# Fused attention and gated FFN on one core: the opening in a new order, with clock fillers that read a constant

## The chip, the cores and the metric

The kernel runs on one core of one Trainium2 chip. The metric is the device time of one execution in microseconds (us). A profiled execution also has a span, which runs from its first to its last recorded event; the span is about 1.8 us shorter than the time of the same execution.

Single executions of one kernel scatter by some 0.3 us (standard deviation; one of 33 of the kernel before, at 226.29 us, lies farther off).

## The reference, cut to what matters

```
xread = softmax(x @ state.T / 8) @ state       # B=8, H=8, S=512, D=64
sread = softmax(state @ x.T / 8) @ x           # 32 state rows per head
x2    = concat(xread, sread) as (8 * 544, 512) rows
out   = (relu(x2 @ w_gate) * (x2 @ w_val)) @ w_out    # 512 -> 1536 -> 512
```

The result is float32. The products are computed in bfloat16.

## The kernel before

The kernel doesn't compute `xread` and then multiply it by the weights. For each batch it first builds `U`, the state times the gate and value weights, in units of 128, 256 or 512 weight columns. It then multiplies `U` by the transposed attention `ans`. One such "slice" is a batch and 128 of the 1536 inner columns: two gate products and two value products of 512 columns on TensorE (`gv`), a relu on ScalarE, and a multiply on VectorE. The output products (`o`) follow.

```
def u_unit(b, w, lo):                    # 512 columns of one weight, two PSUM banks
    ps = held["u", b, w, lo] = [bank("up"), bank("up")]
    u_mm(ps, b, w, lo, 512)
def c_unit(b, lo, n):                    # 128 or 256 columns, gate then value
    ps = [bank("upc")...  for kc in range(NK)]
    for w in range(2):
        u_mm([p[:, w] for p in ps], b, w, lo, n)
def gv(b, jf):
    held["gv", b, jf] = [bank("gv_ps"), bank("gv_ps")], hsb[b][:, jf], S
    for w in range(2):
        for kc in range(NK):
            gv_mm(held["gv", b, jf][0], b, jf, w, kc)
def mult(b, jf):                         # VectorE; frees the value bank
    nc.vector.tensor_tensor(out=dst, in0=ps[1][:, 0:n], in1=held["g", b, jf][:, 0:n], op=ALU.mult)
def att_scale(b, jp, eng="dve"):         # VectorE; both inputs in SBUF
    ...tensor_tensor(out=<a_sn>, in0=<e_sn>, in1=held["rc", b, jp].to_broadcast(...), op=ALU.mult)
def x_next(b):                           # GpSimd casts a whole batch of x, in two halves
    x_conv(b, 0, "pool")
    x_conv(b, 1, "pool")
    x_trans_dma(b)
def spin(n, cols=512):                   # fillers: keep TensorE busy while data is on its way
    for i in range(n):
        nc.tensor.matmul(warm_ps[:, 0:cols], warm[:, 0:128], warm[:, 0:cols], start=True, stop=True)
...
nc.vector.memset(warm, 0.0)
```

The first 28 slices, with all loads, transposes and `U` units among them, are issued by a hand-written program of words. Each engine takes its own words in the order given. `gv.1.8@21` is a slice (batch 1, inner part 8) whose gate goes to PSUM bank 2 and whose value goes to bank 1. `co`/`uo` are copies of `U` units out of PSUM, `nx` is `att_scale`, `xn` is `x_next`, `dw` are weight loads, and `sr` is the state read, on which nothing of the next slices depends. From slice 28 on a loop takes over, in both kernels the same.

The softmax here doesn't subtract the row's maximum and nothing guards it: scores larger than these inputs give would overflow.

## Time and profile before

| | before |
|---|---|
| time, median of 3 | 224.28 us (224.14 to 224.79) |
| the profiled execution | 224.73 us, span 222.9 us |
| TensorE busy | 217.4 us, 98% of the span |
| TensorE on the chain that ended last | 95% |
| full clock from | 10.21 us |
| first gate product | 15.12 us |
| start of slice 28, the loop's first | 56.44 us |

TensorE has almost no idle time after the first gate product, so the date of slice 28 decides the end. Behind it both kernels issue the same stream, and the span moves by what slice 28 moves, unless a later wait absorbs it. The prediction below shows the page, the chain and the timeline from which this is read. Columns: start, length, engine, line, operation, out<-in, sizes, count, and in brackets the idle time before and what ended it.

```profile
17.05 0.29 PE L291 MATMUL upc<-wv_sb,stT 64*32 64x256 bf16 x8
...
39.73 0.68 DVE L219 TENSOR_TENSOR a_sn<-e_sn,rc 128x512 bf16<-128x512 bf16 x1
40.70 2.02 POOL L142 CAST xb<-xf 128x1024 bf16<-128x1024 f32 x2 [4.96 <-DMA xf<-in_x_dram]
```

The value weights landed at 15.41 us and were wanted at 17.05, so they were early. The product took 0.68 us and was over 0.29 us before the two casts began.

### The profile page before, as it was taken

Reading aid. Unit: us, or ns where it says so; the run is one execution under the profiler, and the core shown is the slowest. Engines: PE = TensorE matmul, PEld = TensorE weight load, DVE = VectorE, ACT = ScalarE, POOL = GpSimd, SP = SyncE. Lnnn points to the kernel's source line nnn. Section 1 sums busy time; section 2 is a strip of 40 time slices with the busy share of each in tenths; the row PEclk is TensorE's granted clock in tenths of the full one; section 3 lists DMA queues with packets and bytes.
Section 4 is the critical chain, followed back from the end, with each engine's and each line's share of the span. In section 5 each row is a group of like instructions: output and inputs, shape, how many; then the busy total and the mean of one; then the engine's idle time right before and its main releaser. Section 6 shows DMA issues by size and latency. Waiting matters only on the chain.

```text
span 222.9 us, 4842 instructions
## 1 busy us (share of the span) xinstructions
PE 217.4 (98%) x1959; PEld 106.9 (48%) x1959; DVE 131.1 (59%) x233; ACT 123.2 (55%) x233; POOL 48.9 (22%) x54
## 2 busy tenths in 40 slices
PE   6999999999999999999999999999999999999994
PEld 2554454444544444444444444444444445666543
DVE  2399998965695559664877368646875433222100
ACT  4498788843567555574466456645654444222221
POOL 8877654300603334015000700000000000000000
PEclk9999999999999999999999999999999999999999
DMA  6999999152046771771169114511311111111132
GB/s 154 183 195 197 208 232 284 39 121 97 0 124 209 119 260 62 164 247 50 50 134 281 56 50 97 97 47 47 94 50 47 47 49 50 49 69 72 51 94 94
DMA packets 37799, 25.48 MB, mean 114 GB/s; under 512 B 18864, under 2 KB 33200, under 8 KB 37776
## 3 DMA queue, kind: packets, MB, share of 16 engines
q1 hardware_dynamic: 24912, 16.85, 26.3%
q0 software_dynamic: 11968, 7.47, 21.5%
q10 hardware_dynamic: 896, 0.85, 1.5%
q8 instruction: 15, 0.25, 0.4%
q14 instruction: 8, 0.07, 0.1%
HBM read 18.35 MB, written 8.91 MB: 122 GB/s over the span
## 4 chain that ended last, share of the span: by engine, by line
PE 95%; ACT 2%; DMA 1%; issue 0%; DVE 0%; DVEq 0%; ACTq 0%
PE o_ps L353 39%; PE gv_ps L316 38%; PE gv_ps L333 5%; PE up L291 4%; PE sc_ps L200 2%; DMA st_f<-in_state_dram 1%; PE sr_ps L264 1%; PE upc L291 1%; PE o_ps L379 1%; PE warm_ps L432 1%; PE xT_ps L186 1%; PE stT_ps L129 1%; PE xT_ps L169 1%; PE xT_ps L173 0%; ACT xT L189 0%; ACT e_sn L207 0%
## 5 line engine op out<-in xcount | busy, mean ns | idle before, releaser
L316 PE MATMUL gv_ps<-ans,U 128*128 128x512 bf16 x384 | 94.6, 379 | 0.3 <-ACT ans L249 0.3
L353 PE MATMUL o_ps<-wo_sb,h_sb 128*128 128x512 bf16 x372 | 94.8, 379 | 0.0
L340 ACT ACTIVATE g_sb<-gv_ps 128x512 bf16<-128x512 f32 (+1 forms) x108 | 62.5, 581 | 50.1 <-PE gv_ps L316 39.1
L344 DVE TENSOR_TENSOR h_sb<-gv_ps,g_sb 128x512 bf16<-128x512 f32 x96 | 64.7, 688 | 41.5 <-ACT g_sb L340 40.7
L316 PEld LDWEIGHTS <-U 128*128 128x128 bf16 x384 | 36.1, 98 | 40.7 <-issue 0.9
L353 PEld LDWEIGHTS <-h_sb 128*128 128x128 bf16 x372 | 35.3, 98 | 40.0 <-issue 1.6
L361 ACT COPY o_sb<-o_ps 128x512 f32<-128x512 f32 x29 | 17.1, 590 | 16.2 <-PE o_ps L353 16.2
L301 ACT CAST U<-up 128x512 bf16<-128x512 f32 x37 | 19.2, 594 | 11.1 <-PE up L291 11.1
L301 DVE CAST U<-up 128x512 bf16<-128x512 f32 x35 | 22.0, 682 | 2.3 <-PE up L291 1.9
L142 POOL CAST xb<-xf 128x1024 bf16<-128x1024 f32 x10 | 10.1, 1042 | 55.7 <-DMA xf<-in_x_dram 48.4
L256 POOL COPY xa<-xb 128x2048 bf16<-128x2048 bf16 (+1 forms) x9 | 15.6, 1748 | 13.9 <-issue 13.7
L213 DVE TENSOR_REDUCE cs<-e_sn 128x16 f32<-128x512 bf16 x16 | 10.9, 678 | 8.9 <-ACT e_sn L207 8.9
L344 DVE TENSOR_TENSOR hs_sb<-gv_ps,g_sb 128x256 bf16<-128x256 f32 x12 | 5.1, 425 | 15.3 <-PE gv_ps L333 10.5
L207 ACT ACTIVATE e_sn<-sc_ps 128x512 bf16<-128x512 f32 x16 | 9.7, 604 | 4.7 <-PE sc_ps L200 4.6
L219 DVE TENSOR_TENSOR a_sn<-e_sn,rc 128x512 bf16<-128x512 bf16 x16 | 11.4, 723 | 0.3
L291 PEld LDWEIGHTS <-stT 64*32 64x32 bf16 x512 | 5.9, 90 | 9.5 <-issue 8.1
L311 ACT CAST U<-upc 128x512 bf16<-128x512 f32 (+1 forms) x18 | 8.7, 542 | 0.9 <-PE upc L291 0.9
L200 PEld LDWEIGHTS <-xT 128*128 128x128 bf16 x128 | 5.9, 102 | 3.7 <-ACT xT L189 0.4
L291 PE MATMUL up<-wg_sb,stT 64*32 64x512 bf16 x144 | 7.5, 381 | 0.0
L432 PE MATMUL warm_ps<-hs_sb 128*128 128x512 bf16 x15 | 6.2, 548 | 1.2 <-DVE hs_sb L396 1.2
L333 PE MATMUL gv_ps<-br,wg_sb 128*128 128x256 bf16 x48 | 7.2, 273 | 0.0
L333 PE MATMUL gv_ps<-br,wv_sb 128*128 128x256 bf16 x48 | 7.2, 273 | 0.0
(65 smaller groups left out, 126.9 us busy)
## 6 DMA issues: line engine op xcount, KB each, us to landing
out_dram<-o_sb SPq DMA_DIRECT2D x31, 256.0 KB, 2.4
xf<-in_x_dram SPq DMA_DIRECT2D x4, 1024.0 KB, 6.1
wo_sb<-in_moe_w_out_dram POOLq DMA_DIRECT2D x2, 768.0 KB, 14.7
wg_sb<-in_moe_w_gate_dram POOLq DMA_DIRECT2D x5, 256.0 KB, 8.7
wv_sb<-in_moe_w_val_dram POOLq DMA_DIRECT2D x5, 256.0 KB, 9.3
xf<-in_x_dram POOLq DMA_DIRECT2D x1, 1024.0 KB, 15.4
xb<-in_x_dram POOLq DMA_DIRECT2D x3, 256.0 KB, 6.0
xb<-in_x_dram POOLq DMA_DIRECT2D x1, 512.0 KB, 11.7
```

Of the source, the lines that this page charges most:

```text
L200: nc.tensor.matmul(ps[:, :, c, jj], xT[b][:, c, 2 * jp + jj], stT[:, b, 2 * jp + jj], start=True, stop=True)
L213: nc.vector.reduce_sum(out=cs, in_=e_v, axis=AX.X)
L219: {"dve": nc.vector, "pool": nc.gpsimd}[eng].tensor_tensor(out=by_pair(a_sn[b], jp).rearrange("p r (j n) -> p r j n", n=Ns), in0=e_v, in1= ...
L256: nc.gpsimd.tensor_copy(out=v[:, hs:hs + src.shape[1]], in_=src)
L291: nc.tensor.matmul(dst[parity][32 * j:32 * j + 32], stT[r:r + 64, b, j, 32 * parity:32 * parity + 32], wsb[r:r + 64, j, lo:lo + n], start= ...
L301: copy[eng](out=U[b][:, w, kc, lo:lo + 512], in_=held["u", b, w, lo][kc])
L316: nc.tensor.matmul(ps[w], U[b][:, w, kc, f0:f0 + 128], ANS[b][:, kc].rearrange("p c t -> p (c t)"), start=(kc == 0), stop=(kc == NK - 1))
L333: nc.tensor.matmul(ps[w][:, 0:nt], wsb[:, j, f0:f0 + 128], br[:, j].rearrange("p b n -> p (b n)"), start=(j == 0), stop=(j == NJ - 1))
L340: nc.scalar.activation(out=g_sb[:, 0:n], in_=ps[0][:, 0:n], func=AF.Relu)
L344: nc.vector.tensor_tensor(out=dst, in0=ps[1][:, 0:n], in1=held["g", b, jf][:, 0:n], op=ALU.mult)
L353: nc.tensor.matmul(held["o", b, tsub], src[:, jf, tsub * 128:(tsub + 1) * 128], wo_sb[:, jf], start=(jf == 0), stop=(jf == NF - 1))
L361: copy[eng](out=o_sb, in_=held["o", b, tsub])
```

## The change

The intent is an earlier start. The fillers no longer wait for a memset, since they read a constant of ones that is there from the beginning, broadcast from one column. Some have 256 columns, to fit smaller gaps. And the words of the first 28 slices are put into a new order, made for the durations as they now are. `turn` only sets which bank the loop's outputs begin with.

```
-    warm = hs_sb.rearrange("p f n -> p (f n)")[:, 0:512]
-    given, turn = [], {"r": 0, "o": 0}
+    given, turn = [], {"r": 0, "o": 1}
-    nc.vector.memset(warm, 0.0)
+    one = nc.const_aps.tensor(1.0, (128, 1), BF16)
-            nc.tensor.matmul(warm_ps[:, 0:cols], warm[:, 0:128], warm[:, 0:cols], start=True, stop=True)
+            nc.tensor.matmul(warm_ps[:, 0:cols], one.to_broadcast([128, 128]), one.to_broadcast([128, cols]), start=True, stop=True)
     program = """
-    dx.1.0.2 dx.1.1.2 stc.0.0.act stc.0.1.dve xc.0.0.act dw.0.0.128 spin.6 stT.0@5 xT.0.0@0 ...
+    dx.1.0.2 dx.1.1.2 stc.0.0.act stc.0.1.dve dw.0.0.128 xc.0.0.dve spin.8 xT.0.0@0 ...
     (cut: words up to the second slice)
-    gv.0.1@42 ... c.0.256.256@17 c.1.256.256@65 co.0.256.256.1.act co.0.256.256.0.dve aT.1.0@3 aT.1.1@4 ...
+    gv.0.1@53 ... c.0.256.256@67 co.1.128.128.0.act aT.1.0@0 ... c.1.256.256@15 aT.1.1@4 ...
     (cut: words of slices 2 to 19)
-    ... nx.2.0 ... sc.2.1@5 o.0.1 uo.2.0.512.0.act xn.3 ...
+    ... nr.2.0 gv.1.8@21 ex.2.1 xn.3 re.1.8 nx.2.0 o.0.2 mu.1.8 u.2.0.0@04 of.0.0.act nr.2.1 u.2.1.0@35 u.2.1.512@21 ...
     (cut: words of slices 21 to 26)
-    gv.2.3@23 mu.2.1 re.2.3 o.0.9@7 mu.2.3 sr.0@4 sr.1@5 sn.0 sn.1 xp.2 xp.3
+    ... o.0.9@6 mu.2.2 u.2.0.512@42 sr.0@3 uo.2.0.512.1.act sr.1@5 sn.0 uo.2.0.512.0.act sn.1 xp.2 xp.3
```

More of the change, by code (lines that the diff above doesn't have):

```diff
@@ L441 @@
     program = """
-    dx.1.0.2 dx.1.1.2 stc.0.0.act stc.0.1.dve xc.0.0.act dw.0.0.128 spin.6 stT.0@5 xT.0.0@0 xc.0.1.dve dw.1.0.128 on
-    sto.0.dve xT.0.1@4 xo.0.0.dve dw.0.128.128 xo.0.1.act dw.1.128.128 dw.0.256.256 spin.4 xT.0.3@2 dw.1.256.256
-    xT.0.2@3 xo.0.3.dve sc.0.0@1 xo.0.2.act ex.0.0 sc.0.1@6 dw.0.512.256 xT2.1.0@5 ex.0.1 nr.0.0 xo2.1.0.act
-    dw.1.512.256 spin.2 xT2.1.1@0 nr.0.1 xo2.1.1.act sc.1.0@4 dw.0.768.256 nx.0.0 dw.1.768.256 ex.1.0 spin.2
-    c.1.0.128@23 nx.0.1 sc.1.1@1 co.1.0.128.1.act c.0.0.128@65 co.1.0.128.0.dve dw.0.1024.256 aT.0.1@0 ex.1.1
@@ L447 @@
-    co.0.0.128.0.dve aT.0.0@4 co.0.0.128.1.act ao.0.1.dve dw.1.1024.256 ao.0.0.act spin.1 c.1.128.128@32 nr.1.1
-    c.0.128.128@16 co.1.128.128.1.act gv.0.0@50 co.0.128.128.0.act nr.1.0 co.0.128.128.1.act dw.0.1280.256 re.0.0
-    gv.0.1@42 co.1.128.128.0.act nx.1.1 re.0.1 nx.1.0 dw.1.1280.256 c.0.256.256@17 c.1.256.256@65 co.0.256.256.1.act
-    co.0.256.256.0.dve aT.1.0@3 aT.1.1@4 co.1.256.256.0.act ao.1.0.dve gv.0.2@71 dx.2.0.1 ao.1.1.dve
-    co.1.256.256.1.act mu.0.1 re.0.2 gv.1.0@36 mu.0.0 ds re.1.0 mu.0.2 c.1.512.256@45 c.0.512.256@27
@@ L452 @@
-    co.1.512.256.0.act co.1.512.256.1.dve gv.1.1@03 co.0.512.256.1.act do.0.6 co.0.512.256.0.dve re.1.1 gv.1.4@14
-    mu.1.0 xp.0 re.1.4 gv.1.3@57 mu.1.1 re.1.3 mu.1.4 gv.0.5@20 mu.1.3 do.6.12 re.0.5 gv.0.3@61 mu.0.5 xp.1 re.0.3
-    c.0.768.256@35 c.0.1024.256@47 mu.0.3 co.0.768.256.1.act gv.1.2@20 co.0.1024.256.1.act co.0.768.256.0.dve df.3
-    re.1.2 gv.0.4@61 co.0.1024.256.0.dve re.0.4 mu.1.2 gv.1.5@57 mu.0.4 re.1.5 gv.0.9@32 mu.1.5 re.0.9 gv.0.8@46
-    mu.0.9 re.0.8 c.1.1280.256@01 c.0.1280.256@57 mu.0.8 co.1.1280.256.1.act xT2.2.1@3 co.0.1280.256.1.act
@@ L457 @@
-    co.1.1280.256.0.dve xT2.2.0@2 stc.1.0.pool co.0.1280.256.0.act c.1.768.256@46 xo2.2.1.dve stc.1.1.pool
-    c.1.1024.256@17 xo2.2.0.act stc.3.0.pool gv.1.10@05 co.1.768.256.0.dve stc.2.0.pool co.1.768.256.1.dve
-    co.1.1024.256.1.act stc.2.1.pool stT.1@3 gv.1.11@42 stc.3.1.pool re.1.10 sto.1.dve co.1.1024.256.0.act mu.1.10
-    gv.0.11@76 re.1.11 re.0.11 mu.1.11 gv.1.7@30 mu.0.11 re.1.7 gv.1.9@15 mu.1.7 re.1.9 sc.2.0@4 gv.0.7@72 mu.1.9
-    ex.2.0 re.0.7 nr.2.0 gv.0.6@36 re.0.6 mu.0.7 gv.0.10@01 mu.0.6 re.0.10 u.2.0.0@45 u.2.1.512@73 nx.2.0
@@ L462 @@
-    uo.2.0.0.1.act u.2.0.512@20 o.0.0@6 mu.0.10 uo.2.0.512.1.act uo.2.1.512.0.act uo.2.0.0.0.dve sc.2.1@5 o.0.1
-    uo.2.0.512.0.act xn.3 uo.2.1.512.1.dve ex.2.1 u.2.1.1024@01 nr.2.1 u.2.1.0@42 uo.2.1.1024.0.act u.2.0.1024@35
-    o.0.2 uo.2.1.0.1.act uo.2.0.1024.1.dve uo.2.1.0.0.act o.0.3@7 nx.2.1 of.0.0.dve aT.2.1@0 gv.1.8@25
-    uo.2.1.1024.1.dve ao.2.1.act re.1.8 uo.2.0.1024.0.dve aT.2.0@4 o.0.4 ao.2.0.dve mu.1.8 gv.2.0@01 re.2.0 o.0.5
-    mu.2.0 gv.2.2@23 of.0.1.act re.2.2 gv.1.6@45 mu.2.2 re.1.6 o.0.6@6 mu.1.6 o.0.7 o.0.8 gv.2.1@01 of.0.2.dve re.2.1
@@ L467 @@
-    gv.2.3@23 mu.2.1 re.2.3 o.0.9@7 mu.2.3 sr.0@4 sr.1@5 sn.0 sn.1 xp.2 xp.3
+    dx.1.0.2 dx.1.1.2 stc.0.0.act stc.0.1.dve dw.0.0.128 xc.0.0.dve spin.8 xT.0.0@0 xc.0.1.dve dw.1.0.128 on
+    xo.0.0.dve spin.1.256 xT.0.1@2 dw.0.128.128 stT.0@1 xo.0.1.act dw.1.128.128 sto.0.dve spin.1 spin.1.256 sc.0.0@3
+    dw.0.256.256 xT.0.2@5 ex.0.0 xT.0.3@4 dw.1.256.256 xo.0.2.dve xo.0.3.act nr.0.0 dw.0.512.256 spin.2 sc.0.1@6
+    xT2.1.0@0 ex.0.1 nx.0.0 xo2.1.0.act nr.0.1 dw.1.512.256 spin.2 xT2.1.1@2 xo2.1.1.act dw.0.768.256 sc.1.0@1 nx.0.1
@@ new lines @@
+    dw.1.768.256 spin.1 c.0.0.128@35 ex.1.0 aT.0.0@4 co.0.0.128.0.dve sc.1.1@6 co.0.0.128.1.act ao.0.0.dve aT.0.1@0
+    dw.0.1024.256 ex.1.1 c.1.0.128@21 nr.1.0 ao.0.1.act dw.1.1024.256 spin.1 c.0.128.128@35 c.1.128.128@46
+    co.1.0.128.0.act nr.1.1 co.0.128.128.1.act spin.2 gv.0.0@02 co.0.128.128.0.act co.1.128.128.1.act nx.1.0
+    dw.0.1280.256 re.0.0 gv.0.1@53 nx.1.1 co.1.0.128.1.act re.0.1 mu.0.0 dw.1.1280.256 c.0.256.256@67
+    co.1.128.128.0.act aT.1.0@0 co.0.256.256.0.act co.0.256.256.1.dve c.1.256.256@15 aT.1.1@4 ao.1.0.dve
@@ new lines @@
+    co.1.256.256.1.act gv.0.2@26 dx.2.0.1 mu.0.1 ao.1.1.act co.1.256.256.0.act gv.0.3@70 re.0.2 ds gv.1.2@53 re.0.3
+    mu.0.2 re.1.2 mu.0.3 c.1.512.256@41 do.0.6 c.0.512.256@27 co.1.512.256.1.act mu.1.2 gv.1.1@65 co.0.512.256.1.act
+    xp.0 co.1.512.256.0.dve re.1.1 gv.1.0@01 co.0.512.256.0.dve re.1.0 mu.1.1 c.0.768.256@37 c.1.768.256@46 do.6.12
+    gv.1.5@20 mu.1.0 co.1.768.256.1.act co.1.768.256.0.dve re.1.5 xp.1 gv.1.4@51 co.0.768.256.0.dve re.1.4 gv.1.3@62
+    co.0.768.256.1.dve re.1.3 mu.1.4 df.3 gv.1.7@43 mu.1.5 re.1.7 gv.0.4@57 mu.1.3 re.0.4 mu.1.7 gv.0.5@61 mu.0.4
@@ new lines @@
+    re.0.5 gv.0.7@04 mu.0.5 re.0.7 c.1.1280.256@25 c.0.1280.256@37 mu.0.7 co.1.1280.256.1.act c.0.1024.256@61
+    xT2.2.0@0 co.0.1024.256.0.act co.0.1024.256.1.dve xT2.2.1@4 co.0.1280.256.0.act stc.1.0.pool co.0.1280.256.1.dve
+    gv.0.9@56 xo2.2.0.act xo2.2.1.dve stc.1.1.pool gv.0.6@13 co.1.1280.256.0.dve re.0.9 re.0.6 stc.2.0.pool mu.0.9
+    gv.0.8@74 mu.0.6 re.0.8 stc.3.0.pool gv.0.11@05 mu.0.8 re.0.11 stc.2.1.pool gv.1.6@21 mu.0.11 re.1.6 stc.3.1.pool
+    stT.1@6 gv.0.10@73 mu.1.6 sto.1.act re.0.10 c.1.1024.256@40 u.2.1.1024@52 mu.0.10 co.1.1024.256.1.act
@@ new lines @@
+    u.2.0.1024@61 o.0.0@7 co.1.1024.256.0.act uo.2.1.1024.0.dve uo.2.1.1024.1.act uo.2.0.1024.0.dve gv.1.10@03
+    uo.2.0.1024.1.act re.1.10 sc.2.0@4 o.0.1 ex.2.0 mu.1.10 sc.2.1@5 nr.2.0 gv.1.8@21 ex.2.1 xn.3 re.1.8 nx.2.0 o.0.2
+    mu.1.8 u.2.0.0@04 of.0.0.act nr.2.1 u.2.1.0@35 u.2.1.512@21 uo.2.0.0.0.act o.0.3@6 uo.2.1.512.1.act uo.2.0.0.1.dve
+    uo.2.1.512.0.act o.0.4 nx.2.1 uo.2.1.0.0.act aT.2.1@0 uo.2.1.0.1.act aT.2.0@1 ao.2.1.dve o.0.5 ao.2.0.act
+    gv.2.0@42 of.0.1.act re.2.0 o.0.6@7 mu.2.0 gv.1.11@35 re.1.11 o.0.7 mu.1.11 gv.2.3@01 re.2.3 gv.2.1@42 mu.2.3
@@ L468 @@
+    re.2.1 o.0.8 mu.2.1 gv.1.9@35 of.0.2.dve re.1.9 gv.2.2@01 mu.1.9 re.2.2 o.0.9@6 mu.2.2 u.2.0.512@42 sr.0@3
+    uo.2.0.512.1.act sr.1@5 sn.0 uo.2.0.512.0.act sn.1 xp.2 xp.3
     """
```

## The prediction

> **What bounds the kernel now.** I read the page first, then the chain of waits in order of time, then the timeline of the first 18 us, because the change touches nothing after the first 28 slices but what these leave behind. The page:
>
> ```profile
> PE 217.4 (98%) x1959; PEld 106.9 (48%) x1959; DVE 131.1 (59%) x233; ACT 123.2 (55%) x233; POOL 48.9 (22%) x54
> PE 95%; ACT 2%; DMA 1%; issue 0%; DVE 0%; DVEq 0%; ACTq 0%
> ```
>
> TensorE is the engine of the end, busy 98% of the span and 95% of the chain that ended last. A busy figure with modelled ends can hide stalls, so I compared the start-to-start times of its products with the 216 ns that a 512-column product takes when full (20 in 4.42 us, below). From 15.12 us to the end I find three sorts of excess only: about 93 ns at each change between full products and those on part of the array, one wait of 0.20 us at 17.9 us, and the last output. So every microsecond by which the first gate product (line 316) comes sooner is a microsecond of the end, unless a later wait takes it back. The chain in time:
>
> ```profile
> 0.72 3.17 DMA st_f<-in_state_dram
> 4.54 0.61 PE stT_ps L129 x4
> 5.16 1.16 PE xT_ps L169 x8
> 6.32 1.71 PE warm_ps L432 x4
> 8.03 1.02 PE xT_ps L173 x9
> 9.71 0.61 PE sc_ps L200 x8
> 12.03 1.01 ACT xT L189
> 15.12 1.89 PE gv_ps L316 x8
> 20.62 4.42 PE gv_ps L316 x20
> ```
>
> Four fillers stand on the chain at 6.32 us, ahead of transposes whose input had landed (the transfer's semaphore is complete at 6.83 us). Later ScalarE carries the chain. The timeline of its first part:
>
> ```profile
> 1.18 2.74 PE L432 MATMUL warm_ps<-hs_sb 128*128 128x512 bf16 x6 [1.18 <-DVE hs_sb L396]
> 4.54 0.61 PE L129 MATMUL stT_ps<-id,st_b 128*128 128x128 bf16 x4 [0.63 <-ACT st_b L121]
> 7.96 1.06 PE L173 MATMUL xT_ps<-id,xb 128*64 128x128 bf16 x16
> 10.24 0.64 PE L186 MATMUL xT_ps<-id,xb 128*64 128x128 bf16 x16
> 10.93 2.12 ACT L189 COPY xT<-xT_ps 128x1024 bf16<-128x1024 bf16 x2
> 14.42 0.64 ACT L249 COPY ans<-aT_ps 128x512 bf16<-128x512 bf16 x1
> 15.12 1.89 PE L316 MATMUL gv_ps<-ans,U 128*128 128x512 bf16 x8 [0.26 <-ACT ans L249]
> ```
>
> The six fillers start after the memset, 427 ns apart: half speed. The same 16 transposes take 1.06 us at 7.96 us and 0.64 us at 10.24 us: full speed begins between them, and the trace's clock record puts it at 10.21 us.
>
> **What the Trainium skill says.** "TensorE: Matmul & The Clock Gate", Part 1, What's actually happening: the array runs at half clock until an activity window of some 3.4 us, free-running, was busy. The trace agrees in kind: half speed to 10.21 us, and a full-speed stretch of 211.63 us, 62 windows of 3.413 us. If the windows end at 3.4, 6.8 and 10.2 us here, the products' own time (427 ns a filler, 107 ns a transpose at half speed) covers some 65%, 68% and 85% of them; only the third released the clock, so the limit would lie between 68% and 85% in this run. Part 4 of that page, PE-mode transpose, says that transposes do not count as busy in the same way; without them the third window would be no fuller than the first, so this trace speaks for their counting. The page's head table gives ScalarE and VectorE a strictly ordered queue; the trace agrees, both carry out the program's order, and I use that below.
>
> **The change, part by part.**
> 1. Memset gone. VectorE loses 0.27 us. The fillers can start when the engines are released, about 0.8 us (VectorE's memset stands at 0.85), instead of 1.18. Eight of 427 ns end near 4.2 us, before the first transposes can start at 5.0 us (x lands at 4.47, its cast takes 0.47). So the two extra fillers cost nothing. They lift the coverage of the first window to about 76% ((3.38-0.8)/3.41) and of the second to 75%: inside my uncertain 68 to 85%. I give one half to full speed by 3.4 or 6.8 us.
> 2. Order up to the first gate product. The work ahead of it is the same: four score groups, two transposes of x[1], four small U units, two attention transposes. Fillers grow from 15 to 18 units of 512 columns (17 and two halves). The scores of head half 0 now come before the transposes of x's tail: state transposes end near 6.6 us, their copy near 7.2, scores 7.25 (before 8.96). Then, still at half clock, tail transposes to 8.5, ScalarE's exp to 8.5 and its copy of the second x pair to 9.36, second scores 9.4 (before 9.70), exp at 10.1, and the first 1024-element copy on ScalarE starts near 10.6 (before 10.93). From there ScalarE is full to the gate product, before and after: two large copies, two exps, then two small copies and the attention copy before, one small copy after. The timeline shows 4.13 us from 10.93 to 15.06; one small copy less (0.25 us apart) makes 3.85. Gate product at 14.5: 0.65 us sooner. With the clock released by 6.8 us the tail transposes end near 7.7, the second scores come at 8.5, the copy at 9.6, and the gate product at 13.5: 1.6 us sooner, of which some 0.15 us goes to the 256-column value weights that land at 15.41 us and would be wanted at 15.2.
> 3. From there to slice 28. Same 28 gate/value pairs and ten output parts. Changes between part-array and full-array work rise by my count from 16 to 18: +0.19 us. The wait of 0.20 us at 17.9 us probably goes: -0.20. The third x lands at 29.19 us; with 0.41 us of U work and changes moved ahead of it, its transposes are wanted at 30.05 or 29.3, so it just fits.
> 4. The hand-over. The new program ends with the U unit of batch 2, gate, columns 512, then two state-read groups (sr), and the first slice of the loop reads exactly those columns. In the built order this slice waits on ScalarE, which makes both copies, that of row half 1 first. For such a unit the timeline shows 39.56 us for its first product, and:
>
> ```profile
> 40.06 2.05 ACT L301 CAST U<-up 128x512 bf16<-128x512 f32 x4 [0.23 <-PE up L291]
> 55.81 0.71 PE L264 MATMUL sr_ps<-xa,e_sn 128*32 128x65 bf16 x64
> 56.45 1.04 PE L316 MATMUL gv_ps<-ans,U 128*128 128x512 bf16 x4
> ```
>
> The first copy starts 0.50 us after the unit's first product, the second 0.485 us later and takes 0.59: ready at 1.58, seen near 1.64. TensorE reaches the slice at 0.22 (unit) + 0.09 + 0.64 (sr and its change) = 0.95 us. It stands 0.69 us. Before, these columns were copied a dozen us earlier and gv followed sr with no wait. Nothing behind can absorb it: the stream is full to the end.
>
> Sum against the profiled run of 224.73 us, whose clock came late: late again -0.65 +0.19 -0.20 +0.69 = 0.0; early -1.45 +0.19 -0.20 +0.69 = -0.8, or 223.95. The faster runs of before (224.14, 224.28) I read as luckier windows; the change keeps their like at about 224.1.
>
> **Rivals.**
> A. No stall at the hand-over: the copies are in time or the order's author timed them well. Then -0.7 to -1.5: 223.2 to 224.0. Against it: both copies stand on one in-order engine, the first mm waits for the second of them, and an order made for the first 28 slices need not have counted what waits behind.
> B. The start does not move: ScalarE's run of copies or the DMA (busy tenths 9 from the second slice to the sixth) sets the gate product. Then only the additions stay, +0.7: 225.0. For it: ScalarE is busy 4.75 of the 5 us from 10 to 15. Against it: the run's own start moves, since the fillers and tail transposes no longer stand before the first scores.
> C. The fillers cost more: products reading one column over and over may not run at 427 and 216 ns. Eight have 0.8 us to spare, the nine behind have less; at 10% more, 0.2 us.
> D. A full-array product and no data may give a different window; the luck of the window alone moves a run by the 0.65 us that before's three runs span.
>
> **Range and chances.** The two halves of the clock question give 223.95 and 224.1 to 224.7; rival A pulls down, B up; I weigh A a little more, as such an order is usually kept for being faster. Predicted 224.0 us, 8 in 10 from 223.2 to 224.9. A change of 2% is 4.5 us, more than all idle and half-speed time I could remove, the 10.2 us of half clock being mostly waits for data: faster 0.01, within 2% 0.985, slower 0.005.
>
> **What would show it.** Right: fillers from about 0.8 us with no wait; first scores near 7.2 us; first gate product at 13.3 to 14.7 us; a wait of TensorE for ScalarE's U copy of some 0.7 us after sr near 55 us; no other wait beyond 0.3 us. Wrong: a gate product at 15 us or later (part 2), no wait after sr (part 4), new waits for weights or for the third x between 15 and 30 us (part 3), filler spacing off 427 or 216 ns (rival C).

## The result

| | before | after |
|---|---|---|
| time, median of 4 in the same rounds | 224.21 us (224.09 to 224.79) | 225.15 us (224.74 to 225.64) |
| ratio | | 1.0044 (95%: 1.0021 to 1.0067) |
| the profiled execution: time, span | 224.73, 222.9 us | 225.11, 223.3 us |

A ratio is the mean time of one kernel's runs over that of the other's of the same rounds, so it is not quite the ratio of the medians in the table. By the measure of 2% the two are the same. But the change is no gain: it costs something, and 225.15 lies outside the range of the prediction. With all runs together, the 33 of the kernel before have a mean of 224.56 us (median 224.50) and the 10 of the kernel after 225.00 (median 225.09), so the change costs about 0.5 us.

The page after, the lines for busy time and for the chain that ended last:

```profile
PE 213.8 (96%) x1934; PEld 106.1 (48%) x1963; DVE 130.2 (58%) x228; ACT 125.1 (56%) x237; POOL 49.4 (22%) x54
...
PE 85%; DMA 4%; POOL 3%; DVE 3%; issue 2%; ACT 2%; POOLq 0%; DVEq 0%
```

The fall of TensorE's busy time is not real. The trace has all 1963 weight loads and only 1934 products, 29 too few. At 216 ns each that is 6.3 us, more than the fall of 3.6, and each lost record leaves a gap that looks like a wait. A gap of 432 ns between two products' starts must therefore be checked against the weight loads before it is called one. The chain's shares are real news: DMA and VectorE are now on it. The chain after, in order of time:

```profile
7.66 8.38 DMA wv_sb<-in_moe_w_val_dram
17.65 2.32 PE gv_ps L315 x10
...
41.24 1.14 issue
42.38 0.69 DVE h_sb L343
43.67 1.67 PE o_ps L352 x7
```

It comes in by the value weights' transfer, which lands at 16.04 us. Near 41 us it goes over to VectorE: 1.14 us of "issue" (nothing that the profile shows as a wait; VectorE is inside the product `a_sn` then) and a multiply. The timeline of the kernel after says what these are. First the front:

```profile
0.76 3.57 PE L431 MATMUL warm_ps<-const-bfloat16-1.0 128*128 128x512 bf16 x8 [0.76 <-PEq L561]
6.25 0.39 PE L199 MATMUL sc_ps<-stT,xT 128*128 128x64 bf16 x8 [0.19 <-DVE stT L132]
...
13.67 1.89 PE L315 MATMUL gv_ps<-ans,U 128*128 128x512 bf16 x8
...
16.08 0.30 PE L290 MATMUL upc<-wv_sb,stT 64*32 64x256 bf16 x8 [0.28 <-DMA wv_sb<-in_moe_w_val_dram]
```

Eight fillers run from 0.76 us at once, the clock is full from 4.32 us on, and the first gate product comes at 13.67 us, 1.45 us before that of the other profile. Then TensorE comes to the 256-column value weights before they are there. Against its undisturbed course it loses 0.47 us (the bracket counts only idle time after the modelled end). Then the stretch near 42 us:

```profile
40.87 2.48 POOL L141 CAST xb<-xf 128x1024 bf16<-128x1024 f32 x2 [5.07 <-DMA xf<-in_x_dram]
40.98 1.47 DVE L218 TENSOR_TENSOR a_sn<-e_sn,rc 128x512 bf16<-128x512 bf16 x1
...
42.20 0.59 PE L290 MATMUL up<-wv_sb,stT 64*32 64x512 bf16 x9
42.38 0.68 DVE L343 TENSOR_TENSOR h_sb<-gv_ps,g_sb 128x512 bf16<-128x512 f32 x1
...
43.11 0.41 PE L290 MATMUL up<-wv_sb,stT 64*32 64x512 bf16 x7 [0.32 <-DVE h_sb L343]
```

The product `a_sn` now starts while GpSimd casts the fourth batch of x. It takes 1.47 us instead of 0.69. The multiply behind it (`mu.1.8`) is late by as much. That multiply empties bank 1, and the unit `u.2.1.512@21` wants bank 1. So the sixteen products of the two units (9 and 7) take 1.32 us, from 42.20 to 43.52, where 0.6 would do. Measured from start to start, TensorE loses 0.73 us. Last, the hand-over to the loop:

```profile
55.22 0.41 PE L290 MATMUL up<-wg_sb,stT 64*32 64x512 bf16 x8
55.56 0.70 PE L263 MATMUL sr_ps<-xa,e_sn 128*32 128x65 bf16 x64
55.70 1.07 ACT L300 CAST U<-up 128x512 bf16<-128x512 f32 x2 [1.07 <-PE up L290]
...
57.06 0.81 PE L315 MATMUL gv_ps<-ans,U 128*128 128x512 bf16 x3 [0.79 <-ACT U L300]
```

The first loop slice waits for the second of two copies of the unit that was made just before it. Its first product's record is one of the lost ones; its weight load stands at 56.83 us and shows the true start, 0.65 us after the slice could have begun.

From profile to profile the account is then closed (us, up to the start of slice 28):

| term | after minus before |
|---|---|
| first gate product 15.12 to 13.67 | -1.45 |
| wait for the value weights | +0.47 |
| bank wait behind VectorE's late multiply | +0.73 |
| two more changes between full-array and part-array products | +0.19 |
| the wait at 17.9 us of before, gone | -0.20 |
| hand-over wait | +0.65 |
| sum | +0.39 |
| slice 28 (weight loads at 56.44 and 56.83) | +0.39 |

The span differs by 0.38 us. Behind slice 28 nothing is gained or lost.

### The profile page after: what moved, and what is told of

Same layout as the page of the kernel before. It is cut to its first block, busy times and chain, and to the rows that moved or that the text cites. A ratio compares the mean times of both kernels' runs of the same rounds, so it can differ in the third digit from the quotient of the medians.

```text
span 223.3 us, 4821 instructions
## 1 busy us (share of the span) xinstructions
PE 213.8 (96%) x1934; PEld 106.1 (48%) x1963; DVE 130.2 (58%) x228; ACT 125.1 (56%) x237; POOL 49.4 (22%) x54
## 4 chain that ended last, share of the span: by engine, by line
PE 85%; DMA 4%; POOL 3%; DVE 3%; issue 2%; ACT 2%; POOLq 0%; DVEq 0%
PE o_ps L352 37%; PE gv_ps L315 34%; PE gv_ps L332 5%; PE up L290 4%; DMA wv_sb<-in_moe_w_val_dram 4%; DVE h_sb L343 1%; PE o_ps L378 1%; DVE U L310 1%; PE sc_ps L199 1%; PE sr_ps L263 1%; PE upc L290 1%; POOL wg_sb L109 1%; ACT U L300 1%; POOL xb L419 1%; POOL wv_sb L109 1%
## 5 line engine op out<-in xcount | busy, mean ns | idle before, releaser
L315 PE MATMUL gv_ps<-ans,U 128*128 128x512 bf16 x372 | 93.6, 379 | 1.3 <-ACT U L300 0.8
L352 PE MATMUL o_ps<-wo_sb,h_sb 128*128 128x512 bf16 x358 | 92.3, 379 | 1.9 <-issue 1.7
L300 ACT CAST U<-up 128x512 bf16<-128x512 f32 x39 | 20.4, 595 | 12.1 <-PE up L290 12.1
L360 ACT COPY o_sb<-o_ps 128x512 f32<-128x512 f32 x30 | 17.7, 590 | 16.4 <-PE o_ps L352 16.4
L141 POOL CAST xb<-xf 128x1024 bf16<-128x1024 f32 x10 | 10.6, 1088 | 56.3 <-DMA xf<-in_x_dram 36.7
L300 DVE CAST U<-up 128x512 bf16<-128x512 f32 x33 | 20.8, 682 | 2.3 <-PE up L290 1.9
L343 DVE TENSOR_TENSOR hs_sb<-gv_ps,g_sb 128x256 bf16<-128x256 f32 x12 | 5.1, 425 | 15.3 <-PE gv_ps L332 10.5
L218 DVE TENSOR_TENSOR a_sn<-e_sn,rc 128x512 bf16<-128x512 bf16 x16 | 12.3, 774 | 0.4
L290 PE MATMUL up<-wv_sb,stT 64*32 64x512 bf16 x144 | 7.4, 379 | 0.3 <-DVE h_sb L343 0.3
```

The source lines that it names most:

```text
L218: {"dve": nc.vector, "pool": nc.gpsimd}[eng].tensor_tensor(out=by_pair(a_sn[b], jp).rearrange("p r (j n) -> p r j n", n=Ns), in0=e_v, in1= ...
L290: nc.tensor.matmul(dst[parity][32 * j:32 * j + 32], stT[r:r + 64, b, j, 32 * parity:32 * parity + 32], wsb[r:r + 64, j, lo:lo + n], start= ...
L300: copy[eng](out=U[b][:, w, kc, lo:lo + 512], in_=held["u", b, w, lo][kc])
L315: nc.tensor.matmul(ps[w], U[b][:, w, kc, f0:f0 + 128], ANS[b][:, kc].rearrange("p c t -> p (c t)"), start=(kc == 0), stop=(kc == NK - 1))
L352: nc.tensor.matmul(held["o", b, tsub], src[:, jf, tsub * 128:(tsub + 1) * 128], wo_sb[:, jf], start=(jf == 0), stop=(jf == NF - 1))
L360: copy[eng](out=o_sb, in_=held["o", b, tsub])
```

## The experiments

**Theory.** The change's order wins time at the front, and two new waits, at 42 us and at the hand-over, take more than that. **Rivals.** The value weights set the pace, so that the front gain was never to be had. Or the front gain is the clock's luck in one profile of before. Or the new fillers are at fault. Twelve runs were made, in three jobs; the runs of the kernel before that each job shares have medians of 224.62, 224.66 and 224.55 us. The third job (b2_again, f1_again, h1_landed, g2_split) ran on another chip. The kernel before has a mean of 224.57 us in that job and, without the run at 226.29 us, 224.56 us in the other two, so the two chips are level. The table gives for each run the median, the ratio to before with its interval, and from its one profile when the clock was full, when the 256-column value weights landed, and when the first gate product, slice 14 and slice 28 started. Each interval is some 0.25 to 0.6% wide, and the mean of six runs is good to about 0.15 us.

| run | us (runs) | ratio (95%) | clock full | weights | gate | slice 14 | slice 28 |
|---|---|---|---|---|---|---|---|
| before, first profile | 224.21 (4) | | 10.21 | 15.41 | 15.12 | 32.09 | 56.44 |
| b2_again | 224.39 (6) | 0.9994 (0.9981-1.0008) | 4.25 | 16.34 | 13.92 | 31.42 | 56.06 |
| f1_ones8 | 224.56 (6) | 0.9991 (0.9964-1.0019) | 6.26 | 16.29 | 14.12 | 31.37 | 55.77 |
| f1_again | 224.29 (4) | 0.9990 (0.9977-1.0003) | 6.35 | 16.38 | 14.58 | 31.55 | 56.24 |
| after, first profile | 225.15 (4) | 1.0044 (1.0021-1.0067) | 4.32 | 16.04 | 13.67 | 30.80 | 56.83 |
| a2_again | 225.06 (6) | 1.0006 (0.9976-1.0036) | 6.70 | 16.04 | 14.10 | 30.80 | 56.73 |
| f2_memset | 225.18 (6) | 1.0019 (0.9991-1.0048) | 3.86 | 16.62 | 14.28 | 31.39 | 56.71 |
| e1_port | 224.72 (6) | 0.9998 (0.9972-1.0023) | 4.03 | 16.33 | 13.72 | 31.09 | 56.43 |
| e2_hand | 224.63 (6) | 0.9995 (0.9968-1.0022) | 4.83 | 16.14 | 13.68 | 30.90 | 56.37 |
| e3_wait | 225.27 (6) | 1.0026 (1.0000-1.0051) | 4.07 | 16.30 | 14.18 | 31.60 | 56.93 |
| e4_hybrid | 224.69 (6) | 0.9993 (0.9964-1.0022) | 6.37 | 16.38 | 14.33 | 31.85 | 56.72 |
| g1_fixed | 224.41 (6) | 0.9982 (0.9954-1.0010) | 5.68 | 16.53 | 14.53 | 31.83 | 56.64 |
| h1_landed | 224.11 (5) | 0.9987 (0.9974-1.0001) | 4.25 | unused | 13.69 | 30.33 | 55.68 |
| g2_split | 225.31 (6) | 1.0037 (1.0022-1.0053) | 5.99 | 16.42 | 13.59 | 30.87 | 56.81 |

Slice 14 is comparable only among kernels with the same order, since the orders put different work ahead of it. Ahead of slice 28 the work is the same in all.

### e1_port: the casts kept off the product

A small GpSimd copy that reads one column of `a_sn` makes the casts wait until the product is done.

```
+  "pw": lambda b: nc.gpsimd.tensor_copy(out=tiny, in_=a_sn[b][:, 0, 0, 0:1])
-  ... gv.1.8@21 ex.2.1 xn.3 re.1.8 nx.2.0 o.0.2
+  ... gv.1.8@21 ex.2.1 re.1.8 nx.2.0 pw.2 xn.3 o.0.2
```

> The changed kernel, with the two GpSimd casts of the fourth batch's x made to start only after the VectorE product a_sn of batch 2, head half 0 (a one-column GpSimd copy that reads its output stands before them). Theory (GpSimd holds an SBUF port that this two-input VectorE product needs, which makes it 1.47 us instead of 0.69, delays the multiply behind it and so the PSUM bank that the third U unit near 42.4 us waits for): the product takes about 0.7 us again, the wait of TensorE for VectorE at 42.4 us (0.73 us) falls under 0.15 us, and the time drops by 0.6 to 0.7 us from 225.15. Rival (VectorE is simply too full there, the port is no matter): the product still takes over 1.2 us or the wait stays over 0.5 us, time unchanged.

The timeline of e1_port in the same stretch:

```profile
41.28 0.69 DVE L218 TENSOR_TENSOR a_sn<-e_sn,rc 128x512 bf16<-128x512 bf16 x1
...
42.16 2.02 POOL L141 CAST xb<-xf 128x1024 bf16<-128x1024 f32 x2
...
42.49 0.61 PE L290 MATMUL up<-wv_sb,stT 64*32 64x512 bf16 x16
```

The product takes 0.69 us again, and the sixteen `U` products run through in 0.61 us. From slice 14 to slice 28 the profile takes 25.34 us, against 26.03 and 25.93 in the two profiles of the kernel after. So the late product is what made TensorE wait, and the wait is worth 0.6 to 0.7 us of this stretch. The Trainium skill names the mechanism: in "SBUF — State Buffer", Who interferes with whom, it says "A DVE instruction with two SBUF inputs contends with a GpSimd instruction that reads SBUF" (DVE is VectorE). The runs agree. Alone the product takes 0.69 us, beside the casts 1.47. The casts suffer too, 2.48 us for two instead of 2.02. Such a collision does not always cost time: in the loop the first profiles of both kernels have one too (1.37 us at 82.87 us before, 1.31 us at 83.25 us after), and there TensorE does not wait: from its first gate product on no two successive products of the kernel before start more than 0.32 us apart, and the kernel after is as far behind at slice 44 (0.39 us) as at slice 28. It costs where TensorE soon wants the bank behind it. In the time of the whole kernel e1_port has a mean of 224.67 us, 0.33 below the 225.00 of the kernel after. That is no more than the noise allows to call likely.

### e2_hand: the hand-over unit made earlier

```
-  gv.2.2@01 mu.1.9 re.2.2 o.0.9@6 mu.2.2 u.2.0.512@42 sr.0@3 uo.2.0.512.1.act sr.1@5 sn.0 uo.2.0.512.0.act sn.1 ...
+  gv.2.2@01 mu.1.9 u.2.0.512@42 re.2.2 uo.2.0.512.1.act o.0.9@6 mu.2.2 sr.0@3 uo.2.0.512.0.act sr.1@5 sn.0 sn.1 ...
```

> The changed kernel, with the U unit of batch 2, gate, columns 512, one output part earlier (before o.0.9 instead of after it). Theory (the first slice of the loop waits 0.65 us for the second of two ScalarE copies of this unit): the wait after the state-read groups goes to under 0.1 us; one more change between part-array and full-array work costs 0.09 us; time 0.5 to 0.6 us under 225.15. Rival (the slice waits for something else, such as the multiply of slice 27 or a bank): the wait stays over 0.4 us.

The timeline of e2_hand: the slice after the state read, then a stretch 30 us later.

```profile
56.60 0.81 PE L315 MATMUL gv_ps<-ans,U 128*128 128x512 bf16 x3 [0.16 <-issue]
...
85.44 1.90 POOL L255 COPY xa<-xb 128x2048 bf16<-128x2048 bf16 x1
...
86.74 1.14 DVE L218 TENSOR_TENSOR a_sn<-e_sn,rc 128x512 bf16<-128x512 bf16 x1
```

The hand-over wait is gone. The weight load of the slice stands at 56.37 us, 0.46 before that of the kernel after, although the value weights came 0.10 us later in this profile. The bank wait at 42 us stayed (0.70 us), as it should. But this profile gives 0.44 us back: `a_sn` meets another GpSimd instruction at 86.74 us, takes 1.14 us instead of 0.69, and the third `U` unit of that batch waits for it, so that by slice 44 the lead over the kernel after is down from 0.46 to 0.01 us. Removing one wait moved the stream onto the next collision of the same kind. In time, e2_hand has a mean of 224.62 us, 0.38 below the kernel after.

### e3_wait: the wait for the weights filled with other work

Both attention transposes go before the 256-column units, so that TensorE has something to do until the weights land.

```
-  c.0.256.256@67 ... aT.1.0@0 ... c.1.256.256@15 aT.1.1@4 ao.1.0.dve
+  aT.1.0@0 aT.1.1@4 c.0.256.256@67 c.1.256.256@15 ao.1.0.dve
```

> The changed kernel, with both attention transposes of batch 1 ahead of the two 256-column U units instead of between them. Theory (near 15.5 us TensorE waits 0.47 us for value weights that land near 16.0 us, because the front came sooner): the transposes fill 0.45 us of that wait and two changes of array shape (0.19 us) fall away, time 0.4 to 0.6 us under 225.15. Rival (the wait only moves, since ScalarE frees the bank of the second transpose at about 16.0 us, or the slice behind waits for the copies): time within 0.2 us of 225.15.

The timeline of e3_wait:

```profile
16.58 0.38 PE L234 MATMUL aT_ps<-id,a_sn 128*128 128x128 bf16 x4 [0.29 <-ACT U L310]
...
18.01 1.25 PE L315 MATMUL gv_ps<-ans,U 128*128 128x512 bf16 x4 [0.48 <-ACT U L310]
```

The rival was right. The wait for the transfer became two waits for ScalarE's copies: 0.46 us for a bank and 0.55 us for the columns of `U`. The mean of 225.31 us is no better than the kernel after.

### e4_hybrid: the new front, the old middle and end

The words of the kernel after up to its second slice, then those of the kernel before.

```
   (words of the kernel after up to)  mu.0.0 dw.1.1280.256 co.1.128.128.0.act
-  c.0.256.256@67 ... (rest of the kernel after)
+  c.0.256.256@17 c.1.256.256@65 ... (rest of the kernel before, without mu.0.0)
```

> The changed kernel's order up to the second gate product (with its ones fillers), the order of the kernel before from there on. Theory (the front is worth 1.4 us, the loss lies wholly in the order behind it): first gate product near 13.7 us, a weight wait of about 0.3 to 0.5 us near 15.6 us stays, no wait at 42 us nor after the state reads; span about 222.0 us, time 0.7 to 1.2 us under the kernel before (223.0 to 223.5). Rival (the kernel before had another limit, such as the third x or the weights, right behind its front): the gain is under 0.3 us, with new waits between 15 and 31 us.

This is a miss, and the rival came nearer: no gain, and a limit right behind the front. There was no wait at 42 or 56 us, but the first gate product came only at 14.33 us in its profile, because the last part of batch 0 and batch 1 of x landed later. Start to start, against the same order in before's first profile, TensorE then lost 0.38 us at 18.4 us, to a multiply on VectorE, and 0.52 us at 32.7 us. The timeline of e4_hybrid from 30 to 36 us shows the second:

```profile
31.34 5.43 POOL L123 TENSOR_SCALAR st_b<-st_f,odd 128x256 bf16<-128x256 f32 x6 [4.55 <-DMA st_f<-in_state_dram]
...
33.23 0.40 PE L128 MATMUL stT_ps<-id,st_b 128*128 128x128 bf16 x4 [0.34 <-POOL st_b L123]
```

The rest of the state landed at 31.25 us, GpSimd cast it, and TensorE's transposes of it (`stT.1`) wait for the second cast. This is a limit of the old order that stands behind any early front. In its four profiles with an early clock (b2_again, f1_ones8, f1_again, e4_hybrid) the state landed at 30.59, 30.30, 30.77 and 31.25 us, and slice 28 started 25.47 us later in each. The mean is 224.64 us, level with before. An early front put in front of the old order doesn't make it faster.

### a2_again and b2_again: the two kernels once more, unchanged

> The changed kernel once more, unchanged, for a second profile and more times next to the kernel before on the same chip. Four runs each gave 225.15 against 224.21 us, but eleven runs of the kernel before in another job had a median of 224.62. Theory (four waits behind the front cost about 1.85 us and two changes of shape 0.19, the front gives 1.44 and one wait of 0.20 goes): 0.3 to 0.9 us slower than before in the median; the waits near 15.6, 42.4 and 56.2 us are there again with some 0.4 to 0.7 us each. Rival (the difference was a draw of few runs): ratio within 0.1% and one of the three waits missing.

In a2_again the waits at 42 us and at the hand-over are there again, the one at 42 us a little shorter. The third that was expected, for the weights, is down to 0.05 us, because the first gate product came 0.42 us later. Its timeline:

```profile
40.99 1.37 DVE L218 TENSOR_TENSOR a_sn<-e_sn,rc 128x512 bf16<-128x512 bf16 x1
```

The kernel after is 224.89 us in the mean here. The ratio is 1.0006, and with one wait nearly missing that is the sign that had been named for the rival, so this run alone does not show a loss; without before's run at 226.29 us, the ratio would be about 1.001. With the first rounds the kernel after stays about 0.5 us behind before.

> The kernel before once more, for a second profile. Its runs spread from 224.03 to 225.19 us, and the one profile at hand is of a 224.73 us run with full speed only from 10.21 us. Theory (its spread is the clock's release, which moves the first gate product): another release time, and the first gate product moves with it (14.2 to 15.2 us), no wait over 0.25 us behind it, the span shorter by what the gate product is earlier. Rival (the spread is in the transfers): release again near 10 us or gate product at 15.1 us with another span.

The timeline of b2_again, the kernel before in another execution:

```profile
13.92 1.89 PE L316 MATMUL gv_ps<-ans,U 128*128 128x512 bf16 x8 [0.26 <-ACT ans L249]
...
16.38 0.30 PE L291 MATMUL upc<-wv_sb,stT 64*32 64x256 bf16 x8 [0.34 <-DMA wv_sb<-in_moe_w_val_dram]
```

This settles the rival of luck. With the clock full at 4.25 us the unchanged kernel has its first gate product at 13.92 us, 1.20 us before its own first profile and only 0.25 us after the kernel after. It, too, then waits for the value weights, which had not been expected, and at 32.57 us for the cast of the state (see e4_hybrid): of its 1.20 us these take 0.55 and 0.29, and slice 28 starts only 0.38 us sooner. So 1.2 of the 1.45 us of front gain in the account above belong to the execution and not to the change. The late weights, 16.34 us here, are not the change's doing either; 15.41 was the odd value. The remaining 0.25 us is not the change's doing either, by the record: in all thirteen profiles but the first of before, in both orders and with both sorts of fillers, the first gate product stands 3.81 to 3.85 us after the second half of batch 1 of x landed (9.85 us in the kernel after, 10.07 in b2_again). No run moved that transfer on purpose.

### f1_ones8, f1_again and f2_memset: the fillers alone

f1 is the kernel before with fillers of ones, no memset and `spin.8` for `spin.6` (f1_again is the same file once more). f2 is the kernel after with the memset and the zeros of before.

```
f1, from before:  -warm = ...  -nc.vector.memset(warm, 0.0)  +one = nc.const_aps.tensor(1.0, (128, 1), BF16)
                  fillers read one.to_broadcast(...); spin.6 -> spin.8
f2, from after:   +warm = ...  +nc.vector.memset(warm, 0.0)  -one = ...   fillers read warm
```

> The kernel before with its own order, but with the fillers that read ones, no memset, and eight of them first instead of six: the filler part of the change alone. Theory (the early fillers fill the first clock windows, full speed comes at 4 to 6.5 us in place of 10.2): clock release under 7 us, first gate product at 13.9 to 14.6 us instead of 15.12, no new wait at 42 or 56 us, time 0.3 to 0.9 us under the kernel before. Rival (the clock's release is a matter of the window's chance, not of the fillers): release spread up to 10 us, time as before.

> The changed kernel's order with the old fillers (a memset tile, so they start near 1.18 us and eight of them end near 4.6 us). Theory (the order needs the early start: the fillers then reach into the first transposes' time and the clock is released later): first gate product 0.2 to 0.8 us later than 13.67 us; behind it the weight wait near 15.6 us shrinks by as much, so that the end moves by under 0.4 us. Rival (the start of the fillers is off the path): gate product within 0.1 us of 13.67.

> The order of the kernel before with eight early fillers that read ones, again. Its first profile had a span of 222.26 us, its six runs a median of 224.56, so the profile was of its best run. Theory (behind an early clock the value weights pace this order too, with more slack): release under 7 us again, first gate product at 14.0 to 14.6 us, a weight wait of 0 to 0.5 us, and the median within 0.2 us of the kernel before.

The fillers are not at fault. f1 is level with before (means 224.53 and 224.31 us), without the 0.3 to 0.9 us that it was expected to gain, and f2 is no faster than the kernel after (225.16). What the new fillers are worth is not resolved at this noise. In the profiles they make the clock come early with more certainty: in all eleven with fillers of ones it was full between 4.03 and 6.70 us, in the three with the memset at 10.21, 4.25 and 3.86. But three profiles are too few for a rate.

### g1_fixed: both waits removed, and the later collision too

e1_port and e2_hand together, and in the loop the casts are also held behind each batch's last `a_sn` product.

```
+    def pool_after(b, jp=None):
+        nc.gpsimd.tensor_copy(out=tiny, in_=by_pair(a_sn[b], 1 if jp is None else jp)[:, 0, 0:1])
     (program: as e1_port and e2_hand)
+            at(s, 9, pool_after, b)
             at(s, 9, x_next, b + 1)
```

> The changed kernel with both faults mended: the last U unit one output part earlier, and in all batches the GpSimd casts made to start behind the batch's last a_sn product. Theory (the port collision and the late U unit are what the changed kernel loses): no wait over 0.15 us at 42 or 56 us, no a_sn product over 0.75 us from batch 2 on, no wait near 88.6 us (0.44 us in the run with the earlier U unit alone); 0.9 to 1.3 us under the changed kernel's 225.15, so 223.8 to 224.3, and under the kernel before by 0.1 to 0.6 us. Rival (what is taken away at one place comes back at another, as it did with the earlier U unit alone): less than 0.5 us under the changed kernel.

There is no wait at 42, 56 or 88 us. The mean is 224.43 us, 0.57 below the kernel after, short of the 0.9 to 1.3 us expected, and level with before. In its profile the third batch of x landed late (30.77 us against 29.26 in the kernel after) and cost 0.43 us, so its slice 28 stands at 56.64 us. The stretch from slice 14 to slice 28, which holds both waits, took 24.81 us. Sorted by what waits they have, the kernels with this order fall into groups: 24.81 us with neither (g1), 25.32 to 25.47 with one (e1, e2, e3, f2, h1), 25.93 and 26.03 with both (the two profiles of the kernel after). f2, e3 and h1 count as "one" because in their profiles the product happened not to wait for the casts: in h1 these began after it had ended, in f2 0.45 us after it had begun, and in e3 it got in at the end of the first cast, and the second took 1.56 us instead of 1.04.

### h1_landed: the value weights not waited for (wrong result)

The value half of the 256-column units reads columns that landed long before.

```
-            u_mm([p[:, w] for p in ps], b, w, lo, n)
+            u_mm([p[:, w] for p in ps], b, w, 0 if w == 1 and lo == 256 else lo, n)
```

> The changed kernel with the value part of the 256-column U units of batches 0 and 1 computed from value columns 0 to 255, which have landed, instead of 256 to 511: a wrong result on purpose, the same work, no wait for those weights. Theory (in five profiles of the changed order the slice after the first 14 starts 14.76 us after these weights landed, whatever the first gate product did: the weights set the pace): no wait near 15.6 us, that slice starts 0.3 to 0.6 us sooner than with the weights, and the median falls by as much from 225.08 unless the third x, which lands near 29.3 us, catches it. Rival (the front's gain is lost further on anyway, as at the copies or the bank): the median stays within 0.15 us.

The result was wrong as intended (relative error 0.31). The timeline of h1_landed, at the value half of the first unit and in the stretch near 41 us:

```profile
15.63 0.29 PE L290 MATMUL upc<-wv_sb,stT 64*32 64x256 bf16 x8
...
40.52 0.69 DVE L218 TENSOR_TENSOR a_sn<-e_sn,rc 128x512 bf16<-128x512 bf16 x1
41.41 2.02 POOL L141 CAST xb<-xf 128x1024 bf16<-128x1024 f32 x2 [5.64 <-DMA xf<-in_x_dram]
```

With nothing to wait for, slice 14 starts at 30.33 us, 0.47 before that of the kernel after, from the same first gate product (13.69 and 13.67). So the weights do set the pace there. The other side of it is in the table: in after, a2_again, e1_port, e2_hand and f2_memset slice 14 starts 14.76 or 14.77 us after the weights landed, whether the first gate product came at 13.67 or at 14.28 us. The mean of h1 is 224.25 us, 0.75 below the kernel after (measured on the other chip). That is more than the 0.47, and the profile shows why: the product came sooner, the casts began 0.20 us after its end, and the wait at 42 us was gone too. The hand-over wait (0.64 us) stayed.

### g2_split: a correct way around the weights

From g1: the gate halves of both 256-column units first, the value halves later, and the transposes of the third x three slices later.

```
-  c.0.256.256@67 ... aT.1.0@0 co... c.1.256.256@15 aT.1.1@4
+  cg.0.256.256@67 ... cg.1.256.256@15 aT.1.0@0 cv.0.256.256 co... cv.1.256.256 aT.1.1@4
-  xT2.2.0@0 ... xT2.2.1@4  (before gv.0.9)
+  xT2.2.0@2 xT2.2.1@6      (after gv.0.8)
```

> The kernel with both faults mended, and besides the gate parts of the two 256-column units of batches 0 and 1 computed first, the value parts behind the first attention transpose of batch 1, and the third x transposed three slices later. Theory (the value weights and then the third x pace the front): 0.33 us of other work stands in the weight wait, the wait for the third x is gone, median 0.2 to 0.4 us under 224.41, so 224.0 to 224.2. Rival (ScalarE's copies of the units bind at once, as when both transposes were moved ahead): no gain, or up to 0.3 us slower.

The rival was right. The waits moved to ScalarE; the timeline of g2_split shows the largest:

```profile
30.88 2.33 PE L323 MATMUL gv_ps<-ans,U 128*128 128x512 bf16 x9 [0.76 <-ACT U L318]
```

Together with 0.31 us at 15.3 and 0.42 us at 17 they make it slower than before by 0.37%. No version is clearly faster than before.

## Why the prediction was right or wrong, point by point

**What bounds the kernel.** Right. Every microsecond of the account is one of TensorE's stream up to slice 28.

**Part 1, the fillers.** Right. They start at 0.76 us and run at 427 ns; rival C, that they cost more, fell. The even chance for an early clock was too low for this kernel (all eleven profiles with such fillers), and, worse, it was not set against the same chance in the kernel before. The limit of 68 to 85% of a window was tested by no run.

**Part 2, the first gate product.** The early branch was right in size: 13.5 foreseen, 13.67 measured. What failed is the base. The prediction set its terms "against the profiled run of 224.73 us, whose clock came late" and only remarked that the faster runs of before might be luckier. b2_again shows that a lucky run of before has its gate product at 13.92 us. Like against like the front gain was 0.25 us in one pair of profiles, not 1.45, and 0.22 of it is x landing sooner. The path was another too: with an early clock the first gate product followed the landing of batch 1 of x, not a chain that the fillers and the order had shortened. So that 13.5 came close is in part luck.

**Part 3, the value weights.** The mechanism was right and the size was off: foreseen "some 0.15 us", measured 0.47, because the landing time was taken from that same profile (15.41 us), while the twelve other profiles that use them have 16.04 to 16.62. Together with part 2 this makes rival B half right: not ScalarE but transfers pace the front, and all that TensorE gains ahead of them is lost in waiting for them. (Rival B's 225.0 us is reckoned from some 224.3 us, not from the 224.73 us of the other sums.) The two changes of shape (+0.19 us) and the wait at 17.9 us (gone) were right.

**Part 3, "no other wait beyond 0.3 us".** Wrong, and this is the term that was missing: 0.73 us at 42 us. The prediction counted TensorE's work between slices 2 and 28 and checked inputs that come by DMA. It did not follow the PSUM banks back to VectorE, nor look at what GpSimd does beside it. e1_port shows the chain casts, product, multiply, bank, unit by undoing its first link.

**Part 4, the hand-over.** Right: 0.69 us foreseen, 0.65 measured, by the mechanism foreseen, and e2_hand removed it. Rival A fell.

**The sum.** The early branch was -0.8 us and the measured account between the two profiles is +0.4: of the difference of 1.2 us, 0.73 is the missing wait, 0.32 the weights (0.47 for 0.15), 0.15 the first gate product (1.45 us sooner, not 1.6), less 0.04 at the hand-over. Measured against before's typical profile it reads otherwise: slice 28 stands at 56.13 us in the mean of four profiles with before's order (before, b2, f1 twice) and at 56.76 in three with after's order (after, a2, f2). That is 0.63 us later, of the size of the timed 0.5 us. The new order brings two waits of up to 0.73 and 0.65 us, and what it gains elsewhere doesn't pay for them.

**What stays open.** How often the product and the casts collide is not known: the product waited in both profiles of the kernel after and in e2_hand, and not in f2, e3 and h1; it depends on when the fourth batch of x lands against TensorE's date, which varies by some tenths. It also stays open whether e1 or e2 alone is worth more: each is some 0.35 us faster than the kernel after, with a noise of nearly 0.2. Nor is it shown what the rest of the new order is worth. The two profiles of the kernel after, less their two waits of some 1.3 us in all, would start slice 28 near 55.5 us, 0.6 before the old order's mean. But g1_fixed, which has neither wait, started it at 56.64 us with late weights and a late third x, and is level with before in time.

## What to carry to other kernels

One profile is one throw of whatever is random at the start: before counting a change against it, profile the kernel before a second time and take the terms that move (here the clock's release and the landing of x, the state and the weights) from both. When an order is changed, follow each PSUM bank and each SBUF operand back through the engine that frees it, and look at what GpSimd does beside a VectorE product with two SBUF inputs; TensorE may wait for it two steps later. A hand-written opening has to count what the first slice behind it waits for, and removing one such wait shows its gain only where the next transfer or collision lets it through.

## What the Trainium skill lacked or had wrong

- "SBUF — State Buffer", Who interferes with whom, has the contention, and says that whoever comes first keeps the shared pair for a whole instruction. The runs agree (0.69 us alone; 1.47, 1.37 and 1.14 us beside GpSimd), but it gives no cost for a row of casts: here the product got in between two, and the pair of casts grew from 2.02 to 2.48 us.
- "TensorE: Matmul & The Clock Gate", Part 1, What you observe, puts the first release about 4 us into sustained activity, give or take 0.5 us. How far it scatters for an opening with gaps it does not say: the fourteen profiles here have 3.86 to 10.21 us, and the same file 10.21 and 4.25.
- No page that I found has a time for going between full-array products and those on part of the array ("TensorEngine Tiling (Array Packing)", Key Properties, names a drain at a change of tiling mode, without a figure): about 93 ns for each change here, +0.19 us for two more.
- No page that I found says what a product costs whose operands are broadcast from one column: the same 427 ns for 512 columns at half clock as one that reads 512 zeros.
- No page that I found warns of lost product records: 29 of 1963 in one trace, each leaving a gap like a wait of 216 ns.
